# Sparse attention and an FFN on one core: the small attention matmuls issued in six orders of blocks and heads

## The chip, the cores and the metric

The kernel runs on one core of a Trainium2 chip. Its time is the device time in microseconds, the median of several runs. Five engines work side by side, each through its own stream in order: TensorE (matrix products, PE in the profile, with PEld for its weight loads), VectorE (DVE), ScalarE (ACT), GpSimd (POOL) and SyncE (SP, which here only starts DMAs).

## What is computed

Attention over 8 batches, 8 heads, 576 tokens and 64 dimensions a head, with two sparse masks, and then a layer norm with a feed-forward block:

```python
scores = (q @ k.T) / sqrt(64)
mask_local   = (rel >= 0) & (rel < 32)                 # heads 0 to 3
mask_strided = (rel >= 0) & (pos_k % 32 == pos_q % 32) # heads 4 to 7
attn = softmax(where(mask, scores, -1e9))
x = (attn @ v), heads side by side: 8 x 576 x 512
xn = (x - mean(x)) / sqrt(var(x) + 1e-6) * g_ln
out = x + max(xn @ w_ch1, 0) @ w_ch2                   # 512 -> 2048 -> 512
```

## The kernel before

The tokens are worked in nine chunks of 512: one for each batch, and a ninth for the 64 last tokens of all batches. A chunk's FFN is 16 steps (f = 0 to 15). In each step `ffn1` (L748, L755) makes 128 hidden units by 512 tokens, ScalarE and VectorE split them in two parts (`h_high`, `h_low`), and `second` (L775) adds their products into four output banks. The steps are skewed: between `ffn1` of step f and `second` of step f - 1 there is a place for other work on TensorE.

The heads come in pairs, 32 of them, two heads of the same mask in a pair: strided and local pairs alternate. Only the blocks that the mask leaves are computed. A local pair has 18 blocks of 32 queries for each head, a strided pair 11 blocks of three strides (54 queries) for each head. The two heads of a pair lie on different rows of TensorE's array (head 0 on rows 0 to 63, head 1 on rows 64 to 127), and neighbouring blocks of one head on different columns: four groups of 32 columns for local blocks, two groups of 64 for strided ones, used in turn (`tile_position` in L445 and L515). All are plain float32 matmuls; each stands as two load and matmul pairs in TensorE's stream.

Batches 0 and 1 are worked ahead of and within chunk 0, by an order written out by hand (`ORDER`). From chunk 1 on a generator, `pieces`, brings the other 24 pairs, one at every fourth FFN step. Its first part is `m_piece` (L670): in one bank tile `m` of 1536 columns it issues the scores of the next pair (`s_blocks`, L451 to L453, matmul L445), then the v products of this pair (`v_blocks`, L546 to L548, matmul L515). These are called a visit here. VectorE then masks the scores and divides the products, and DMAs carry the softmax weights out and back for the visit after. Both loops run over blocks outside and the two heads inside:

```python
            for i in range(n):
                for h in range(2):
                    block(i, h)
```

The order of instructions within an engine is the order in which the program is written; TensorE's stream is fixed by it.

Of the kernel before, what the change touches and what calls it, by code (L numbers as in the profile page):

```python
# [20 lines left out]
T:0:0:0 T:0:1:1 c:0:0: c:0:1: T:1:0:2 S:0::0 c:1:0: T:1:1:2 mask:0 max:0 T:2:1:0 c:1:1: sub:0  # L21
S:1::1 c:2:1: exp:0 T:2:0:2 mask:1 max:1 PP:0::0 c:2:0: T:3:0:1 sub:1 pt:0 c:3:0: V:0::2 exp:1
vs:1 S:2::0 den:0 xo:0 PP:1::1 mask:2 X:0::2 pt:1 max:2 W:0 T:3:1:0 xh:0 sub:2 V:1::1 xl:0 c:3:1:
S:3::2 den:1 r:4 xo:1 low:0:0 sc:0:0 low:0:1 exp:2 mg:0:0 mask:3 PP:2::1 X:1::0 pt:2 sg:0:0 W:1
max:3 xh:1 V:2::2 sc:0:1 xl:1 sub:3 tp:4 byg:0 exp:3 W:2 PP:3::0 add:0 den:2 S:4::1 pt:3 mg:0:1
vs:3 xo:2 cm:0::0 low:1:0 X:2::2 W:3 mask:4 sg:0:1 V:3::1 xh:2 max:4 sc:1:0 cen:0 sub:4 xl:2 r:5
hi:0:0 lowA:2:0 mg:1:0 hi:0:1 lo:0:0 F:0 exp:4 den:3 sg:1:0 lowA:3:0 lo:0:1 xo:3 sc:1:1 low:1:1
byg:1 X:3::1 mg:1:1 v:4 sg:1:1 add:1 PP:4::2 xh:3 sc:2:0 xl:3 cm:1::0 mg:2:0 Fb:0 pt:4 lowA:3:1
W:4 cen:1 H:0 lowA:2:1 sg:2:0 hi:1:0 tp:5 byg:2 V:4::0 hh:0 sc:2:1 add:2 hl:0 S:5::1 hi:1:1 st:1
mg:2:1 lo:1:0 cm:2::2 sg:2:1 F:1 W:5 mask:5 sc:3:0 lo:1:1 hi:2:1 cen:2 H:1 mg:3:0 hi:2:0 G:0  # L30
sg:3:0 hh:1 den:4 W:6 sc:3:1 hl:1 lowA:4:1 mg:3:1 lo:2:0 byg:3 lowA:4:0 F:2 sg:3:1 add:3 xo:4
sc:4:0 hi:3:1 W:7 mg:4:0 H:2 lo:2:1 lowA:5:0 sg:4:0 cm:3::0 G:1 cen:3 byg:4 sc:4:1 hi:3:0 mg:4:1
add:4 hh:2 sg:4:1 st:4 hl:2 sc:5:0 X:4::0 lo:3:0 F:3 mg:5:0 xh:4 r:6 lo:3:1 lowA:5:1 xl:4 H:3
sg:5:0 cm:4::0 hh:3 G:2 cen:4 byg:5 sc:5:1 hl:3 lowA:6:1 v:5 add:5 mg:5:1 hi:4:0 sg:5:1 lowA:6:0
lo:4:0 F:4 max:5 sc:6:0 lowA:7:0 mg:6:0 sub:5 lowA:7:1 cm:5::0 sg:6:0 H:4 cen:5 W:8 sc:6:1 byg:6
G:3 hh:4 mg:6:1 add:6 hi:4:1 hl:4 hi:5:0 sg:6:1 lo:5:0 cm:6::0 sc:7:0 F:5 cen:6 W:9 exp:5 lo:4:1
mg:7:0 hi:5:1 sg:7:0 H:5 tp:6 byg:7 sc:7:1 PP:5::0 lowA:8:0 G:4 add:7 st:0 hh:5 hi:6:0 hl:5 lo:5:1
pt:5 r:7 mg:7:1 hi:6:1 S:6::0 lo:6:0 sg:7:1 lowA:9:0 lowA:8:1 F:6 mask:6 sc:8:0 max:6 cm:7::0
mg:8:0 sg:8:0 sub:6 H:6 st:3 G:5 hh:6 cen:7 byg:8 st:2 hl:6 hi:7:0 lo:6:1 tp:7 sc:8:1 hi:7:1
V:5::0 add:8 lowA:9:1 r:8 F:7 mg:8:1 sg:8:1 lo:7:0 den:5 sc:9:0 xo:5 H:7 mg:9:0 sg:9:0 cm:8::0  # L40
hh:7 G:6 exp:6 byg:9 hl:7 W:10 sc:9:1 cen:8 add:9 mg:9:1 hi:8:0 PP:6::0 hi:8:1 sg:9:1 lo:8:0 F:8
tp:8 pt:6 W:11 lo:7:1 hi:9:1 cm:9::0 H:8 lo:8:1 sc:10:0 cen:9 lowA:10:0 G:7 lowA:10:1 mg:10:0 W:12
hi:9:0 sg:10:0 hh:8 byg:10 sc:10:1 hl:8 S:8::0 lowA:11:0 lo:9:0 mg:10:1 F:9 lowA:11:1 sg:10:1 v:6
add:10 mask:8 sc:11:0 H:9 mg:11:0 lo:9:1 lowA:12:1 sg:11:0 cm:10::0 G:8 hh:9 cen:10 byg:11 W:13
sc:11:1 hi:10:0 mg:11:1 hi:10:1 lo:10:0 hl:9 lowA:12:0 S:7::0 sg:11:1 add:11 sc:12:0 F:10 mask:7
W:14 lo:10:1 mg:12:0 cm:11::0 sg:12:0 H:10 max:7 sc:12:1 byg:12 G:9 hh:10 cen:11 st:5 add:12
mg:12:1 hi:11:0 hl:10 lowA:13:1 W:15 lo:11:0 sg:12:1 hi:11:1 cm:12::0 F:11 max:8 sc:13:0 lowA:13:0
cen:12 H:11 mg:13:0 hi:12:0 v:7 sg:13:0 lo:12:0 X:5::0 hh:11 G:10 xh:5 lo:11:1 sc:13:1 xl:5
lowA:14:1 hl:11 sub:7 hi:12:1 mg:13:1 V:6::0 lowA:14:0 r:9 byg:13 F:12 sg:13:1 den:6 add:13 xo:6
sc:14:0 H:12 lo:12:1 lowA:15:0 mg:14:0 exp:7 cm:13::0 sg:14:0 G:11 hi:13:1 cen:13 byg:14 xr:0  # L50
hh:12 sc:14:1 hl:12 lo:13:1 hi:13:0 mg:14:1 X:6::0 lo:13:0 sg:14:1 F:13 xh:6 add:14 xr:1 sc:15:0
xl:6 H:13 sub:8 mg:15:0 cm:14::0 hh:13 G:12 cen:14 xr:2 sg:15:0 hi:14:0 hl:13 byg:15 xs:0 PP:7::0
lo:14:0 F:14 pt:7 tp:9 st:6 lowA:15:1 add:15 sc:15:1 H:14 r:10 cm:15::0 hh:14 G:13 cen:15 exp:8
hl:14 hi:14:1 mg:15:1 hi:15:0 sg:15:1 lo:15:0 V:7::0 hi:15:1 xr:3 F:15 lo:15:1 den:7 xo:7 lo:14:1
xs:2 X:7::0 v:8 H:15 G:14 hh:15 xh:7 hl:15 xl:7 v:9 tp:10 PP:8::0 pt:8 xs:3 st:7 r:11 xs:1
# [9 lines left out]
def kernel(  # L65
# [127 lines left out]
    v_l = [v_local(const.tile([P, 4 * NL, D1], F32, name="v_l")),  # L193
           v_local(early.tile([P, 4 * NL, D1], F32, name="v_l1"))]
    v_s = [v_strided(const.tile([P, 2 * NS, D1], F32, name="v_s")),
           v_strided(early.tile([P, 2 * NS, D1], F32, name="v_s1"))]


# [604 lines left out]
    for p in first:  # L803
        if p.k in BY_DVE:
            p.load_qk(early.tile([P, 2 * S], F32, name=f"raw{p.id}"))
        elif p.k == 0:
            for i in range(2):
                p.load_rows(i, nc.sync, slice(0, 1))
                p.load_rows(i, nc.scalar, slice(1, 2))
        else:  # L810
            p.load_rows(0, nc.sync)
            p.load_rows(1, nc.scalar)
    nc.sync.dma_start(gcol, g_ln.rearrange("(c p) -> p c", p=P))
    for p in first:
        p.load_v(once=True)

# [209 lines left out]
```

## Time and profile before

| | |
|---|---|
| median of 3 runs | 906.24 us (904.66 to 908.40) |
| span of the profiled execution | 907.3 us |
| TensorE busy | 884.9 us, 98% of the span |
| VectorE, ScalarE, GpSimd busy | 435.4, 199.7 and 147.9 us |
| DMA | 102.98 MB, mean 114 GB/s |

The span is the time of the profiled execution from its first to its last instruction. A group of instructions is given with its line of the kernel, engine, operation, what it writes and reads, the shape and a count. For a matmul, "64\*32 64x64" means 64 rows by 32 columns of the array and 64 columns streamed. A matmul's busy time reaches from its start to its modelled end, so that neighbours overlap; a row that merges many gives the first start and the time that they cover together. Rates are best read from one row's start to the next.

### The profile page before, as it was taken

The page shows a single profiled execution, that of the slowest core. Times are in us where ns is not written, and L with a number is a line of the kernel's source. Part 1 is how long each engine was busy: PE and PEld are TensorE (multiplying, and loading weights), DVE is VectorE, ACT ScalarE, POOL GpSimd, SP SyncE. Part 2 cuts the span into 40 slices and gives each one's busy share as a digit, 9 for nine tenths or more (in the row PEclk, how much of TensorE's full clock was granted, in tenths as well). Part 3 has the DMA queues.
Part 4 walks back from the last instruction along what each step waited for, and adds up shares of the span by engine and source line. Part 5 has one row for each costly group of instructions (what it writes and reads, how often), then busy time and mean ns, then how long its engine had stood idle before and what let it go on. Part 6 is the DMA issues. An engine that isn't in the chain of part 4 may idle for free.

```text
span 907.3 us, 18531 instructions
## 1 busy us (share of the span) xinstructions
PE 884.9 (98%) x7606; PEld 728.8 (80%) x7606; DVE 435.4 (48%) x864; ACT 199.7 (22%) x326; POOL 147.9 (16%) x186
## 2 busy tenths in 40 slices
PE   7699999999999999999999999999999999999997
PEld 6578787888888888888888888888888888888885
DVE  2888877544654455445644464445533321132113
ACT  3477663111111111111111111111111111111110
POOL 5477774000100011000100010001000000000000
PEclk8999999999999999999999999999999999999999
DMA  8887886675867575766666665757443230002001
GB/s 166 226 257 179 247 196 114 147 111 119 134 142 109 102 137 120 124 91 141 109 134 93 135 104 141 100 127 124 116 85 91 49 128 0 1 1 93 0 1 47
DMA packets 339621, 102.98 MB, mean 114 GB/s; under 512 B 276944, under 2 KB 331344, under 8 KB 339536
## 3 DMA queue, kind: packets, MB, share of 16 engines
q1 hardware_dynamic: 249920, 85.53, 42.9%
q10 hardware_dynamic: 89616, 16.26, 11.5%
q8 instruction: 60, 0.98, 0.5%
q14 instruction: 25, 0.20, 0.1%
HBM read 74.02 MB, written 27.72 MB: 112 GB/s over the span
## 4 chain that ended last, share of the span: by engine, by line
PE 93%; DMA 2%; DVE 1%; issue 1%; SPq 1%; POOL 1%; ACT 0%; DVEq 0%; POOLq 0%; ACTq 0%
PE po L775 42%; PE ph L748 28%; PE ph L755 14%; PE m L515 2%; PE m L445 2%; DMA s<-in_moe_w_ch_dram 1%; PE t L371 1%; PE s L445 1%; DMA rows<-in_q_dram 1%; PE av L515 1%; SPq L351 1%; PE cm L281 1%; PE px L636 0%; PE pp L501 0%; POOL r L270 0%
## 5 line engine op out<-in xcount | busy, mean ns | idle before, releaser
L775 PE MATMUL po<-w,hh 128*128 128x512 f32 x1152 | 359.2, 393 | 0.0
L765 DVE SCALAR_TENSOR_TENSOR hl<-ph,hh 128x512 fp32r<-128x512 f32 x144 | 99.3, 690 | 367.0 <-ACT hh L760 367.0
L775 PEld LDWEIGHTS po<-w,hh 128*128 128x128 f32 x1152 | 213.4, 188 | 44.8
L748 PE MATMUL ph<-xh,w 128*128 128x512 f32 x576 | 226.0, 392 | 1.4 <-ACT w L294 1.2
L775 PE MATMUL po<-w,hl 128*128 128x512 f32 x576 | 224.5, 390 | 0.0
L748 PE MATMUL ph<-xl,w 128*128 128x512 f32 x576 | 224.5, 390 | 0.0
L760 ACT ACTIVATE hh<-ph 128x512 fp32r<-128x512 f32 x144 | 86.1, 598 | 483.7 <-PE ph L755 469.0
L755 PE MATMUL ph<-xh,w 128*128 128x512 f32 x576 | 155.3, 392 | 0.0
L748 PEld LDWEIGHTS ph<-xh,w 128*128 128x128 f32 x576 | 108.3, 188 | 24.1 <-ACT w L294 1.4
L775 PEld LDWEIGHTS po<-w,hl 128*128 128x128 f32 x576 | 108.1, 188 | 23.1
L755 PEld LDWEIGHTS ph<-xh,w 128*128 128x128 f32 x576 | 108.2, 189 | 22.5 <-POOL w L298 0.2
L748 PEld LDWEIGHTS ph<-xl,w 128*128 128x128 f32 x576 | 108.3, 188 | 22.0
L491 POOL TENSOR_TENSOR sm<-sm,mx 128x648 f32<-128x648 f32 (+1 forms) x32 | 40.6, 1269 | 440.4 <-DVE mx L486 440.4
L723 POOL TENSOR_TENSOR rs<-rs,mhalf 128x1 f32<-128x1 f32 x36 | 19.7, 548 | 286.5 <-DVE rs L722 286.5
L497 ACT ACTIVATE sm<-sm 128x648 f32<-128x648 f32 (+1 forms) x32 | 23.8, 742 | 104.3 <-POOL sm L491 104.3
L298 POOL TENSOR_TENSOR w<-r,w 128x512 fp32r<-128x512 f32 x32 | 41.1, 1297 | 7.3 <-ACT w L294 6.9
L687 DVE TENSOR_TENSOR xl<-xo,xh 128x512 fp32r<-128x512 f32 x24 | 16.6, 692 | 38.8 <-ACT xh L686 38.8
L686 ACT ACTIVATE xh<-xo 128x512 fp32r<-128x512 f32 x24 | 15.2, 632 | 62.0 <-DMA pd<-sm 18.2
L486 DVE TENSOR_REDUCE mx<-sm 128x12 f32<-128x648 f32 (+1 forms) x32 | 26.3, 822 | 2.1
L565 DVE TENSOR_TENSOR xo<-m,den 64x64 f32<-64x64 f32 (+3 forms) x120 | 27.1, 289 | 0.0
L781 DVE SCALAR_TENSOR_TENSOR x<-po,rs,x 128x512 f32<-128x512 f32 x36 | 24.5, 737 | 2.0 <-PE po L775 1.8
L718 DVE BATCH_NORM_STATS2 st<-x 128x6 f32<-128x512 f32 x36 | 24.3, 674 | 0.0
(95 smaller groups left out, 561.0 us busy)
## 6 DMA issues: line engine op xcount, KB each, us to landing
s<-in_moe_w_ch_dram SPq DMA_DIRECT2D x32, 512.0 KB
out_dram<-x SPq DMA_DIRECT2D x32, 256.0 KB
raw<-in_q_dram SPq DMA_DIRECT2D x112, 72.0 KB
raw<-in_k_dram SPq DMA_DIRECT2D x112, 72.0 KB
xds<-xo SPq DMA_DIRECT2D x32, 162.0 KB
v_l<-in_v_dram SPq DMA_DIRECT2D x32, 144.0 KB
pd<-sm SPq DMA_DIRECT2D x44, 96.0 KB
pt<-pd ACTq DMA_DIRECT2D x44, 96.0 KB
```

Source lines behind the costliest of these rows:

```text
L298: nc.gpsimd.tensor_tensor(out=t[:, 1], in0=self.w[i], in1=t[:, 0].bitcast(F32), op=ALU.subtract)
L445: nc.tensor.matmul(o, lhsT, rhs, start=True, stop=True, tile_position=(64 * h, pos))
L486: nc.vector.reduce_max(mx[:, :, 0:nt], sm, axis=AX.X)
L491: nc.gpsimd.tensor_tensor(out=sm, in0=sm, in1=mx[:, :, 0:nt].unsqueeze(3).broadcast_to([P, 2, nt, sm.shape[3]]), op=ALU.subtract)
L515: nc.tensor.matmul(at(h, t)[m * j:m * (j + 1)], self.p_cols(rows, t, j), self.v[rows, n, 0:w], start=True, stop=True, tile_position=(64 * ...
L565: nc.vector.tensor_tensor(out=xo[r, t0:t1, h0:h1].rearrange("p t h d -> p h t d"), in0=av, in1=den[r, h0:h1, t0:t1].unsqueeze(3).broadcast_to(
L748: nc.tensor.matmul(ph, w1h[:, cc], x[:, cc, :], start=(new and n == 0 and i == 0), stop=False)
L755: nc.tensor.matmul(ph, w1l[:, cc], xt[c][0][:, cc, :], start=False, stop=(cc == NCC - 1))
L760: nc.scalar.activation(out=hh, in_=ph, func=AF.Relu)
L765: nc.vector.scalar_tensor_tensor(out=hl, in0=ph, scalar=0.0, in1=hh.bitcast(F32), op0=ALU.max, op1=ALU.subtract)
L775: nc.tensor.matmul(po[i], hx[:, cs], w, start=(f == 0 and n == 0), stop=(f == NFC - 1 and n == 2))
L781: nc.vector.scalar_tensor_tensor(out=x, in0=po[i], scalar=rs, in1=x, op0=ALU.mult, op1=ALU.add)
```

## The change

A function `turns(n, kind)` gives the order of the visits to (block, head) in one of six kinds, and the two loops go by it. The kind follows from the number of the pair: visits 0 and 1 have kind 0, visits 2 and 3 kind 1, and so on; after kind 5 it starts again, so that each kind has four of the 24 visits. Kind 0 is the order before. Kind 1 takes two blocks of head 0 and then the same two of head 1; kind 2 alternates heads and crosses the blocks; kind 3 takes four and four; kind 4 all blocks of head 0 and then all of head 1; in kind 5 head 1 follows two blocks behind head 0. Batches 0 and 1 keep kind 0.

```diff
+    def turns(n, kind):
+
+        g = (1, 2, 2, 4, n, 1)[kind]
+        if kind == 5:
+            return [x for i in range(n + 2) for x in ((i, 0), (i - 2, 1)) if 0 <= x[0] < n]
+        out = []
+        for i in range(0, n, g):
+            js = range(i, min(i + g, n))
+            if kind == 2 and len(js) == 2:
+                out += [(i, 0), (i + 1, 1), (i + 1, 0), (i, 1)]
+            else:
+                out += [(j, h) for h in range(2) for j in js]
+        return out
...
-            for i in range(n):
-                for h in range(2):
-                    block(i, h)
+            for i, h in turns(n, (self.k - 9) // 2 % 6 if wide or ps.shape[1] > 1024 else 0):
+                block(i, h)
...
-            for i in range(NB if self.local else NG):
-                for h in range(2):
-                    self.v_block(i, h, lambda h, t: ps[:, o(h, t):o(h, t) + D], D)
+            for i, h in turns(NB if self.local else NG, (self.k - 8) // 2 % 6):
+                self.v_block(i, h, lambda h, t: ps[:, o(h, t):o(h, t) + D], D)
```

The rest of the diff turns the first loads and memsets, which stood as plain lines, into words of `ORDER` at the same place, and gives some steps a choice of engine that no word uses. The other engines' instructions stand in the same order and number as before; so do TensorE's groups of instructions, and what moves is inside a visit. It can be seen where a wait marks a block.

TensorE, visit 8 (the first of kind 4), before: the scores of a local pair and the v products of a strided one, with the FFN's matmuls around them (`m` is the bank tile, `pt` the softmax weights, `v_s` the values, DMAHW the landing of DMAs):

```order
L755 MATMUL ph_0_4151<-xh_3391,w_0_831 128x512 x4
L445 MATMUL m_2_4168<-kt_l,qt_l 32x64 [waits PE_49]
L445 MATMUL m_2_4168<-kt_l,qt_l 32x64 x35
L515 MATMUL m_2_4168<-v_s,pt_2_4088 64x64 [waits DMAHW5_49,DMAHW6_49,DMAHW3_49,DMAHW1_49]
L515 MATMUL m_2_4168<-v_s,pt_2_4088 64x64 [waits DMAHW2_49,DMAHW0_49]
L515 MATMUL m_2_4168<-v_s,pt_2_4088 64x64 [waits DMAHW7_49,DMAHW5_49]
L515 MATMUL m_2_4168<-v_s,pt_2_4088 64x64 x19
```

The same visit now:

```order
L461 MATMUL m_2_4168<-kt_l,qt_l 32x64 x35
L529 MATMUL m_2_4168<-v_s,pt_2_4088 64x64 [waits DMAHW5_49,DMAHW6_49,DMAHW3_49,DMAHW1_49]
L529 MATMUL m_2_4168<-v_s,pt_2_4088 64x64 [waits DMAHW7_49,DMAHW5_49]
L529 MATMUL m_2_4168<-v_s,pt_2_4088 64x64 x9
L529 MATMUL m_2_4168<-v_s,pt_2_4088 64x64 [waits DMAHW2_49,DMAHW0_49]
L529 MATMUL m_2_4168<-v_s,pt_2_4088 64x64 x10
```

Head 1's first block, the one with the wait for DMAHW2 and 0, stood second and stands twelfth, behind all of head 0's.

TensorE, visit 9 (the second of kind 4), before: the scores of a strided pair, the v products of a local one, and the first FFN matmul after them (`kt_s`, `qt_s` hold k and q):

```order
L445 MATMUL m_0_4404<-kt_s,qt_s 64x54 x21
L515 MATMUL m_0_4404<-v_l,pt_0_4339 32x64 [waits DMAHW4_49]
L515 MATMUL m_0_4404<-v_l,pt_0_4339 32x64 [waits DMAHW6_49]
L515 MATMUL m_0_4404<-v_l,pt_0_4339 32x64 x34
L775 MATMUL po_0_4308<-w_3_1071,hh_3_4371 128x512 [waits Activation_49]
```

And now:

```order
L461 MATMUL m_0_4404<-kt_s,qt_s 64x54 x21
L529 MATMUL m_0_4404<-v_l,pt_0_4339 32x64 [waits DMAHW4_49]
L529 MATMUL m_0_4404<-v_l,pt_0_4339 32x64 x17
L529 MATMUL m_0_4404<-v_l,pt_0_4339 32x64 [waits DMAHW6_49]
L529 MATMUL m_0_4404<-v_l,pt_0_4339 32x64 x17
L798 MATMUL po_0_4308<-w_3_1071,hh_3_4371 128x512 [waits Activation_49]
```

The block with the wait for DMAHW6 is head 1's first: it stood second and stands nineteenth.

## Rows read from the trace of the kernel before

**Rows 1.** The page: busy time by engine, and the last chain's shares.
```profile
PE 884.9 (98%) x7606; PEld 728.8 (80%) x7606; DVE 435.4 (48%) x864; ACT 199.7 (22%) x326; POOL 147.9 (16%) x186
...
PE 93%; DMA 2%; DVE 1%; issue 1%; SPq 1%; POOL 1%; ACT 0%; DVEq 0%; POOLq 0%; ACTq 0%
```

**Rows 2.** Busy time in chunks 1 to 6: stretch, length, engines, clock, DMA.
```profile
153.00:703.00 550.00, 550.00 (x4959) 452.58 (x4957) 275.55 (x573) 87.45 (x140) 41.25 (x45) 1.00 0.64 118
```

**Rows 3.** Timeline of TensorE, three visits: start, busy us, line, operation, count.
```profile
156.12 0.92 PE L515 MATMUL m<-v_s,pt 54*64 54x64 f32 x44
156.96 0.74 PE L775 MATMUL po<-w,hh 128*128 128x512 f32 x2
...
416.83 0.91 PE L445 MATMUL m<-kt_s,qt_s 64*64 64x54 f32 x44
417.67 0.97 PE L515 MATMUL m<-v_l,pt 64*32 64x64 f32 x72
418.57 0.73 PE L775 MATMUL po<-w,hh 128*128 128x512 f32 x2
...
440.56 0.97 PE L445 MATMUL m<-kt_l,qt_l 64*32 64x64 f32 x72
441.46 1.07 PE L515 MATMUL m<-v_s,pt 54*64 54x64 f32 x44
442.46 0.74 PE L775 MATMUL po<-w,hh 128*128 128x512 f32 x2
```

**Rows 4.** Groups of TensorE by form, 153 to 703 us: the visits' matmuls.
```profile
L515 PE MATMUL m<-v_s,pt 54*64 54x64 f32 x528 | 12.1, 223 | 0.0
L445 PE MATMUL m<-kt_l,qt_l 64*32 64x64 f32 x864 | 11.7, 224 | 0.0
L515 PE MATMUL m<-v_l,pt 64*32 64x64 f32 x864 | 11.7, 224 | 0.0
L445 PE MATMUL m<-kt_s,qt_s 64*64 64x54 f32 x484 | 10.0, 222 | 0.0
```

**Rows 5.** Timeline, loads, windows from 416.8 to 416.88, 416.90, 417.11 and 417.40.
```profile
416.83 0.15 PEld L445 LDWEIGHTS m<-kt_s,qt_s 64*64 64x64 f32 x4 [0.35 <-issue]
416.83 0.20 PEld L445 LDWEIGHTS m<-kt_s,qt_s 64*64 64x64 f32 x7 [0.35 <-issue]
416.83 0.38 PEld L445 LDWEIGHTS m<-kt_s,qt_s 64*64 64x64 f32 x20 [0.35 <-issue]
416.83 0.68 PEld L445 LDWEIGHTS m<-kt_s,qt_s 64*64 64x64 f32 x40 [0.35 <-issue]
```

**Rows 6.** Timeline, matmuls, windows from 440.5 to 440.62, 440.80, 440.88 and 441.20.
```profile
440.56 0.29 PE L445 MATMUL m<-kt_l,qt_l 64*32 64x64 f32 x8
440.56 0.46 PE L445 MATMUL m<-kt_l,qt_l 64*32 64x64 f32 x32
440.56 0.48 PE L445 MATMUL m<-kt_l,qt_l 64*32 64x64 f32 x33
440.56 0.84 PE L445 MATMUL m<-kt_l,qt_l 64*32 64x64 f32 x65
```

**Rows 7.** Timeline, q's transposes: loads to 25.83 and 25.87, then all matmuls.
```profile
25.79 0.14 PEld L371 LDWEIGHTS t<-ident,rows 96*64 96x64 f32 x2 [0.17 <-DVE sm L473]
25.79 0.20 PEld L371 LDWEIGHTS t<-ident,rows 96*64 96x64 f32 x4 [0.17 <-DVE sm L473]
...
25.79 1.21 PE L371 MATMUL t<-ident,rows 96*64 96x96 f32 x24
26.93 0.45 PE L515 MATMUL av<-v_l,pt 64*32 64x65 f32 x28
```

**Rows 8.** Full-array transposes in the timeline; L515's wait instructions (min/median/max ns).
```profile
25.02 0.85 PE L636 MATMUL px<-ident,xo 128*128 128x128 f32 x6 [0.38 <-DVE xo L565]
...
L515 PEldq EVENT_SEMAPHORE  x68: 51/51/1436, 21.1 to 698.4; - x68
```

More of the change, by code (lines that the diff above doesn't have):

```diff
@@ L20 @@
 ORDER = """
[L21 to L55, printed above, removed]
-"""
-BY_DVE = ()
@@ L59 @@
-ONCE = False
+vm R:0:0 R:0:1 R:1:0 R:1:1:1 R:2:0 R:2:1:1 R:3:0 R:3:1:1 g:0 v:0 v:1 v:2 v:3 T:0:0:0 T:0:1:1 c:0:0:
+c:0:1: T:1:0:2 S:0::0 c:1:0: T:1:1:2 mask:0 max:0 T:2:1:0 c:1:1: sub:0 S:1::1 c:2:1: exp:0 T:2:0:2
+mask:1 max:1 PP:0::0 c:2:0: T:3:0:1 sub:1 pt:0 c:3:0: V:0::2 exp:1 vs:1 S:2::0 den:0 xo:0 PP:1::1
+mask:2 X:0::2 pt:1 max:2 W:0 T:3:1:0 xh:0 sub:2 V:1::1 xl:0 c:3:1: S:3::2 den:1 r:4 xo:1 low:0:0
+sc:0:0 low:0:1 exp:2 mg:0:0 mask:3 PP:2::1 X:1::0 pt:2 sg:0:0 W:1 max:3 xh:1 V:2::2 sc:0:1 xl:1
@@ new lines @@
+sub:3 tp:4 byg:0 exp:3 W:2 PP:3::0 add:0 den:2 S:4::1 pt:3 mg:0:1 vs:3 xo:2 cm:0::0 low:1:0 X:2::2
+W:3 mask:4 sg:0:1 V:3::1 xh:2 max:4 sc:1:0 cen:0 sub:4 xl:2 r:5 hi:0:0 lowA:2:0 mg:1:0 hi:0:1 lo:0:0
+F:0 exp:4 den:3 sg:1:0 lowA:3:0 lo:0:1 xo:3 sc:1:1 low:1:1 byg:1 X:3::1 mg:1:1 v:4 sg:1:1 add:1
+PP:4::2 xh:3 sc:2:0 xl:3 cm:1::0 mg:2:0 Fb:0 pt:4 lowA:3:1 W:4 cen:1 H:0 lowA:2:1 sg:2:0 hi:1:0 tp:5
+byg:2 V:4::0 hh:0 sc:2:1 add:2 hl:0 S:5::1 hi:1:1 st:1 mg:2:1 lo:1:0 cm:2::2 sg:2:1 F:1 W:5 mask:5
@@ new lines @@
+sc:3:0 lo:1:1 hi:2:1 cen:2 H:1 mg:3:0 hi:2:0 G:0 sg:3:0 hh:1 den:4 W:6 sc:3:1 hl:1 lowA:4:1 mg:3:1
+lo:2:0 byg:3 lowA:4:0 F:2 sg:3:1 add:3 xo:4 sc:4:0 hi:3:1 W:7 mg:4:0 H:2 lo:2:1 lowA:5:0 sg:4:0
+cm:3::0 G:1 cen:3 byg:4 sc:4:1 hi:3:0 mg:4:1 add:4 hh:2 sg:4:1 st:4 hl:2 sc:5:0 X:4::0 lo:3:0 F:3
+mg:5:0 xh:4 r:6 lo:3:1 lowA:5:1 xl:4 H:3 sg:5:0 cm:4::0 hh:3 G:2 cen:4 byg:5 sc:5:1 hl:3 lowA:6:1
+v:5 add:5 mg:5:1 hi:4:0 sg:5:1 lowA:6:0 lo:4:0 F:4 max:5 sc:6:0 lowA:7:0 mg:6:0 sub:5 lowA:7:1
+cm:5::0 sg:6:0 H:4 cen:5 W:8 sc:6:1 byg:6 G:3 hh:4 mg:6:1 add:6 hi:4:1 hl:4 hi:5:0 sg:6:1 lo:5:0
@@ new lines @@
+cm:6::0 sc:7:0 F:5 cen:6 W:9 exp:5 lo:4:1 mg:7:0 hi:5:1 sg:7:0 H:5 tp:6 byg:7 sc:7:1 PP:5::0
+lowA:8:0 G:4 add:7 st:0 hh:5 hi:6:0 hl:5 lo:5:1 pt:5 r:7 mg:7:1 hi:6:1 S:6::0 lo:6:0 sg:7:1 lowA:9:0
+lowA:8:1 F:6 mask:6 sc:8:0 max:6 cm:7::0 mg:8:0 sg:8:0 sub:6 H:6 st:3 G:5 hh:6 cen:7 byg:8 st:2 hl:6
+hi:7:0 lo:6:1 tp:7 sc:8:1 hi:7:1 V:5::0 add:8 lowA:9:1 r:8 F:7 mg:8:1 sg:8:1 lo:7:0 den:5 sc:9:0
+xo:5 H:7 mg:9:0 sg:9:0 cm:8::0 hh:7 G:6 exp:6 byg:9 hl:7 W:10 sc:9:1 cen:8 add:9 mg:9:1 hi:8:0
+PP:6::0 hi:8:1 sg:9:1 lo:8:0 F:8 tp:8 pt:6 W:11 lo:7:1 hi:9:1 cm:9::0 H:8 lo:8:1 sc:10:0 cen:9
@@ new lines @@
+lowA:10:0 G:7 lowA:10:1 mg:10:0 W:12 hi:9:0 sg:10:0 hh:8 byg:10 sc:10:1 hl:8 S:8::0 lowA:11:0 lo:9:0
+mg:10:1 F:9 lowA:11:1 sg:10:1 v:6 add:10 mask:8 sc:11:0 H:9 mg:11:0 lo:9:1 lowA:12:1 sg:11:0
+cm:10::0 G:8 hh:9 cen:10 byg:11 W:13 sc:11:1 hi:10:0 mg:11:1 hi:10:1 lo:10:0 hl:9 lowA:12:0 S:7::0
+sg:11:1 add:11 sc:12:0 F:10 mask:7 W:14 lo:10:1 mg:12:0 cm:11::0 sg:12:0 H:10 max:7 sc:12:1 byg:12
+G:9 hh:10 cen:11 st:5 add:12 mg:12:1 hi:11:0 hl:10 lowA:13:1 W:15 lo:11:0 sg:12:1 hi:11:1 cm:12::0
+F:11 max:8 sc:13:0 lowA:13:0 cen:12 H:11 mg:13:0 hi:12:0 v:7 sg:13:0 lo:12:0 X:5::0 hh:11 G:10 xh:5
@@ new lines @@
+lo:11:1 sc:13:1 xl:5 lowA:14:1 hl:11 sub:7 hi:12:1 mg:13:1 V:6::0 lowA:14:0 r:9 byg:13 F:12 sg:13:1
+den:6 add:13 xo:6 sc:14:0 H:12 lo:12:1 lowA:15:0 mg:14:0 exp:7 cm:13::0 sg:14:0 G:11 hi:13:1 cen:13
+byg:14 xr:0 hh:12 sc:14:1 hl:12 lo:13:1 hi:13:0 mg:14:1 X:6::0 lo:13:0 sg:14:1 F:13 xh:6 add:14 xr:1
+sc:15:0 xl:6 H:13 sub:8 mg:15:0 cm:14::0 hh:13 G:12 cen:14 xr:2 sg:15:0 hi:14:0 hl:13 byg:15 xs:0
+PP:7::0 lo:14:0 F:14 pt:7 tp:9 st:6 lowA:15:1 add:15 sc:15:1 H:14 r:10 cm:15::0 hh:14 G:13 cen:15
@@ L60 @@
+exp:8 hl:14 hi:14:1 mg:15:1 hi:15:0 sg:15:1 lo:15:0 V:7::0 hi:15:1 xr:3 F:15 lo:15:1 den:7 xo:7
+lo:14:1 xs:2 X:7::0 v:8 H:15 G:14 hh:15 xh:7 hl:15 xl:7 v:9 tp:10 PP:8::0 pt:8 xs:3 st:7 r:11 xs:1
+"""
 EARLY_F0 = True
@@ L191, in v_strided, with v_frames @@
         return t
[L193 to L196, printed above, removed]
+    v_l = [const.tile([P, 4 * NL, D1], F32, name="v_l"),
+           early.tile([P, 4 * NL, D1], F32, name="v_l1")]
+    v_s = [const.tile([P, 2 * NS, D1], F32, name="v_s"),
+           early.tile([P, 2 * NS, D1], F32, name="v_s1")]
+    def v_frames():
+        for t in v_l:
+            v_local(t)
+        for t in v_s:
+            v_strided(t)
     sms = [const.tile([P, NS, 2, 64], F32, name=f"sm{i}") for i in range(2)]
@@ L266, in sign, with by_g, block_sum @@
                 in1=self.p[i].bitcast(U32), op0=ALU.bitwise_and, op1=ALU.bitwise_or)
-        def by_g(self):
+        def by_g(self, eng):
             self.wg = self.w[0].rearrange("p (c f) -> p c f", c=NCC)
-            nc.gpsimd.tensor_tensor(
+            eng.tensor_tensor(
                 out=self.wg, in0=self.wg, in1=gcol.unsqueeze(2).broadcast_to([P, NCC, P]),
                 op=ALU.mult)
-        def block_sum(self):
-            nc.gpsimd.tensor_tensor(
+        def block_sum(self, eng):
+            eng.tensor_tensor(
                 out=bsum, in0=self.wg[:, 0:2], in1=self.wg[:, 2:4], op=ALU.add)
-            nc.gpsimd.tensor_tensor(out=bsum[:, 0], in0=bsum[:, 0], in1=bsum[:, 1], op=ALU.add)
+            eng.tensor_tensor(out=bsum[:, 0], in0=bsum[:, 0], in1=bsum[:, 1], op=ALU.add)
         def column_mean(self, ps):
@@ L294, in high, with rest @@
             nc.scalar.activation(out=t[:, 0], in_=self.w[i], func=AF.Copy)
-        def rest(self, i):
+        def rest(self, i, eng):
             t = (w1s, w2s)[i][self.f]
-            nc.gpsimd.tensor_tensor(
+            eng.tensor_tensor(
                 out=t[:, 1], in0=self.w[i], in1=t[:, 0].bitcast(F32), op=ALU.subtract)
@@ L316 @@
     NHP = H // 2
+    CC = 2
     CT = 96
-    NA = S // CT // 2
+    NA = S // (CT * CC)
     n_pair = [0, 0]
+    def turns(n, kind):
[10 more added lines that the diff above has]
+        return out
     class Pair:
@@ L358, in load_rows @@
             if self.rows is None:
-                self.rows = early.tile([CT, 2, 2, NA, 2, D], F32, name=f"rows{self.id}")
+                self.rows = early.tile([CT, 2, 2, NA, CC, D], F32, name=f"rows{self.id}")
             src = (q, k)[i]
@@ L363, in load_rows @@
                 src[self.b, self.h0 + hs.start:self.h0 + hs.stop].rearrange(
-                    "h (a p c) d -> p (h a) (c d)", p=CT, c=2))
+                    "h (a p c) d -> p (h a) (c d)", p=CT, c=CC))
         def t_rows(self, i, ps):
@@ L368, in t_rows @@
             for a in range(NA):
-                for c in range(2):
+                for c in range(CC):
                     for h in range(2):
@@ L374, in t_rows, with t_copy @@
             self.t_ps[i] = ps[:, :, 0:2 * CT]
-        def t_copy(self, i):
+        def t_copy(self, i, copy):
             self.qt, self.kt = (qt_l, kt_l) if self.local else (qt_s, kt_s)
@@ L379, in t_copy @@
             if self.local:
-                nc.scalar.copy(
-                    out=dst[:, STR * i:STR * i + S].rearrange("p (a x) -> p a x", a=NA), in_=ps)
-            else:
-                nc.scalar.copy(
-                    out=dst[:, 0:S].rearrange("p (r a u) -> p a u r", a=NA, r=STR),
-                    in_=ps.rearrange("p a (u r) -> p a u r", r=STR))
+                copy(out=dst[:, STR * i:STR * i + S].rearrange("p (a x) -> p a x", a=NA), in_=ps)
+            else:
+                copy(out=dst[:, 0:S].rearrange("p (r a u) -> p a u r", a=NA, r=STR),
+                     in_=ps.rearrange("p a (u r) -> p a u r", r=STR))
         def load_v(self, once=False):
@@ L487, in s_max, with s_sub @@
             self.mx = mx
-        def s_sub(self):
+        def s_sub(self, eng=nc.gpsimd):
             nt, sm, mx = self.nt, self.smv, self.mx
-            nc.gpsimd.tensor_tensor(
+            eng.tensor_tensor(
                 out=sm, in0=sm,
@@ L501, in p_turn, with p_copy @@
                 nc.tensor.transpose(pp[:, P * t:P * (t + 1)], self.sm[:, t].rearrange("p h x -> p (h x)"), ident)
-        def p_copy(self, pp):
+        def p_copy(self, pp, copy):
             pool, tag = (early, f"pt{self.k % 2}") if self.b == 0 else (smp, "pt")
             pt = pool.tile([P, NS, P], F32, tag=tag, name=f"pt{self.id}")
-            nc.scalar.copy(
-                out=pt[:, 0:self.nt].rearrange("p t x -> p (t x)"), in_=pp[:, 0:P * self.nt])
+            copy(out=pt[:, 0:self.nt].rearrange("p t x -> p (t x)"), in_=pp[:, 0:P * self.nt])
             w = STR if self.local else 64
@@ L595, in x_raw, with x_turned, x_blocks, p_turned @@
                     self.xraw[32 * j:32 * j + 32].rearrange("p (g e) -> p g e", e=32), src)
-        def x_blocks(self):
-            xh, xl = x_t(self.b)
-            cc = self.h0 // 2
+        def x_turned(self):
             xT = self.xo.rearrange("p t h d -> p (t h d)")[:, 0:CH]
             nc.vector.transpose(xT, self.xraw)
-            split_x(xh[:, cc, :], xl[:, cc, :], xT)
-        def p_turned(self):
-            nt = self.nt
-            turned = sms[1 - int(self.local)].rearrange("p t h x -> p (t h x)")[
-                :, 0:P * nt].rearrange("p (b t e) -> p b t e", b=4, e=32)
+            cc = self.h0 // 2
+            self.xp = [(xT, *(x[:, cc, :] for x in x_t(self.b)))]
+        def x_blocks(self):
+            self.x_turned()
+            for src, hi, lo in self.xp:
+                split_x(hi, lo, src)
+        def p_turned(self, own=False):
+            nt = self.nt
+            if own:
+                turned = smp.tile([P, NS, P], F32, tag="pt", name=f"turned{self.id}").rearrange(
+                    "p t x -> p (t x)")
+            else:
+                turned = sms[1 - int(self.local)].rearrange("p t h x -> p (t h x)")
+            turned = turned[:, 0:P * nt].rearrange("p (b t e) -> p b t e", b=4, e=32)
             nc.vector.transpose(
@@ L616, in p_turned, with p_load @@
                     turned[32 * j:32 * j + 32].rearrange("p b t e -> p b (t e)"))
-        def p_load(self):
+        def p_load(self, dma=nc.scalar.dma_start):
             nt, src = self.nt, pd[int(self.local)]
@@ L622, in p_load @@
                 ptj = pt.rearrange("p t x -> p (t x)")[:, 0:P * nt]
-                nc.scalar.dma_start(ptj, src.rearrange("p j x -> p (j x)"))
+                dma(ptj, src.rearrange("p j x -> p (j x)"))
                 ptj = ptj.rearrange("p (j t e) -> p j t e", j=4, e=32)
@@ L627, in p_load @@
                 for j in range(4):
-                    nc.scalar.dma_start(
+                    dma(
                         pt[:, 0:nt, 32 * j:32 * j + 32],
@@ L658, in x_parts, with x_high @@
             return [(src, dst(xh), dst(xl)) for src, dst in parts]
-        def x_high(self, px):
-            self.xp = self.x_parts(px)
+        def x_high(self, px=None):
+            if px is not None:
+                self.xp = self.x_parts(px)
             for src, hi, _ in self.xp:
@@ L802 @@
     first = pairs[0:NHP]
[L803 to L815, printed above, removed]
     NP = len(pairs)
@@ L843, in one @@
         p = pairs[k]
-        if op == "T":
+        eng, copy = nc.gpsimd, nc.scalar.copy
+        if op.endswith("D"):
+            op, eng, copy = op[0:-1], nc.vector, nc.vector.tensor_copy
+        if op == "R":
+            if k == 0:
+                p.load_rows(i, nc.sync, slice(0, 1))
+                p.load_rows(i, nc.scalar, slice(1, 2))
+            else:
+                p.load_rows(i, nc.scalar if buf else nc.sync)
+        elif op == "vm":
+            v_frames()
+        elif op == "Z":
+            t = room(f"d{len(ps)}", buf - 1) if buf else wake
+            for _ in range(k):
+                nc.tensor.matmul(
+                    t[:, 0:2 * P].rearrange("p (n x) -> p n x", x=P), mean,
+                    mean.unsqueeze(1).broadcast_to([P, 2, P]), start=True, stop=True)
+        elif op == "g":
+            nc.sync.dma_start(gcol, g_ln.rearrange("(c p) -> p c", p=P))
+        elif op == "T":
             p.t_rows(i, room(f"t{k}{i}", buf))
         elif op == "c":
-            p.t_copy(i)
+            p.t_copy(i, copy)
         elif op == "S":
@@ L854, in one @@
         elif op == "sub":
-            p.s_sub()
+            p.s_sub(eng)
         elif op == "exp":
@@ L860, in one @@
         elif op == "pt":
-            p.p_copy(ps[f"pp{k}"])
+            p.p_copy(ps[f"pp{k}"], copy)
         elif op == "vs":
@@ L874, in one @@
         elif op == "xh":
-            p.x_high(ps[f"px{k}"])
+            p.x_high(ps.get(f"px{k}"))
         elif op == "xl":
             p.x_low()
+        elif op == "pT":
+            p.p_turned(bool(i))
+        elif op == "pL":
+            p.p_load(nc.sync.dma_start)
+        elif op == "xr2":
+            p.x_raw(nc.sync)
+        elif op == "xT":
+            p.x_turned()
         elif op == "tp":
@@ L882, in one @@
         elif op == "v":
-            p.load_v(once=ONCE)
+            p.load_v(once=p.b == 0)
         elif op == "W":
@@ L896, in one @@
         elif op == "byg":
-            split(k).by_g()
+            split(k).by_g(eng)
         elif op == "add":
-            split(k).block_sum()
+            split(k).block_sum(eng)
         elif op == "cm":
@@ L906, in one @@
         elif op == "lo":
-            split(k).rest(i)
+            split(k).rest(i, eng)
         elif op == "F":
```

## The prediction

> **What bounds the kernel now.** I read the chain of work that ended last first: TensorE holds 93% of it [rows 1]. The table by stretches then shows chunks 1 to 6, from 153 to 703 us: TensorE is busy for 550.00 of 550 us, VectorE for half of it, and the granted clock is 1.00, its 2.4 GHz level [rows 2]. In that stage no wait ends last but TensorE's own work, so whatever the change adds to TensorE's stream there is added to the end, and whatever it takes off is taken off. The change touches only the small matmuls of attention. They come in 24 visits of TensorE, one between two halves of each FFN step, and the timeline shows a visit as two rows [rows 3]: the scores of the next pair (L445), then the v products of this pair (L515). Two kinds of block alternate. A "strided" half has 11 blocks for each of two heads, each on 64 rows and 64 columns of the array; a "local" half has 18 for each head on 64 rows and 32 columns. Each float32 block is issued as two load and matmul pairs, so that 22 blocks are x44 and 36 are x72. From row to row a strided half takes 0.84 us (1.00 in most v halves), a local one 0.90 [rows 3]. All 2,740 of these matmuls are 45.5 us of busy time [rows 4]: that is the whole stake, and an order can move a part of it only.
>
> **What paces a visit.** How fast blocks follow each other must be read within a half. In a strided half four loads start, two blocks, one of each head; then nothing starts until between 416.88 and 416.90, some 55 ns after the first at 416.83 [rows 5]. From then on it goes in that step: 20 loads have started by 417.11 and 40 by 417.40, which is 20 loads, five pairs of blocks, in 0.29 us or 58 ns for a pair [rows 5]. Two loads of different heads (other rows of the array) follow within 7 ns or so; the next block of the same head waits 58. In a local half the same step is half as long: 8 matmuls (two blocks of each head) start within 0.06 us, 32 by 0.24 [rows 6], 28 ns for a block of one head. After the 32nd only one starts in the next 0.08 us, and then 32 take 0.32 us [rows 6]: there something other than the array, most likely the supply of instructions, sets the pace at 36 ns for a pair of blocks.
>
> So a head moves on by one block in 58 ns (strided) or 28 ns (local), and the order before runs both heads side by side. Would two blocks of one head also overlap if they are neighbours in the stream? The rows before have one nearby case, the transposes of q and k at L371: their neighbours take the same rows and differ in columns, like block j and block j+1 of one head. Two loads of the first block start at 25.79, and the next two only between 25.83 and 25.87 [rows 7], again the length of one load. A matmul behind a load that cannot start is not passed by others, as far as these rows show: I take it that the stream stops at a block whose head is still loading the block before, even when the block after it belongs to the free head.
>
> **The change, order by order.** Each order serves visits 0 and 1, 2 and 3, and so on, twice in all; two neighbouring visits hold two strided and two local halves, so each order has four of each (order 5 three strided ones, since the last visit has no scores). The order listing shows it where waits mark the blocks: in the first visit of order 4 the wait that head 1's first v block carries moves from the second v block to the twelfth, behind all of head 0. I price a half by its neighbours: 58 (28) ns for a block of the same head as the one before, 14 ns (two pairs at 7) for a block of the other head, and 45 (14) for the last block, whose step no other hides. Before, that gives 11 x 58 = 0.64 us for a strided half; a local one takes the measured 0.75 (0.90 less the 0.15 of changing over, which stays).
> - Order 0 is the order before: 0.
> - Order 1 (two of one head, two of the other): strided 10 x 58 + 12 x 14 + 45 = 0.79, so +0.15; local 18 x 28 + 18 x 14 + 14 = 0.77, so +0.02. Four of each: 0.68 us.
> - Order 2 (heads alternate, columns cross): the heads still alternate, so 0; the odd last block of a strided half meets a column in use, 0 to 58 ns, taken at 30. Four: 0.12 us.
> - Order 3 (four and four): strided 16 x 58 + 6 x 14 + 45 = 1.06, +0.42; local 26 x 28 + 10 x 14 + 14 = 0.88, +0.13. Four of each: 2.2 us.
> - Order 4 (one head, then the other): strided 20 x 58 + 2 x 14 + 45 = 1.23, +0.59; local 34 x 28 + 2 x 14 + 14 = 0.99, +0.24. Four of each: 3.3 us.
> - Order 5 (head 1 two blocks behind): two more steps, 2 x 58 = +0.12 in three strided halves; local 20 x 28 = 0.56 stays under the 0.75 that the supply sets, +0 to 0.05. Together 0.45 us.
>
> The sum is 6.8 us. What works against it: v halves of strided pairs take up to 0.16 us more than the first of them (1.00 against 0.84) [rows 3], since their first blocks wait for several loads, 51 ns for each extra wait instruction [rows 8]; in the head-by-head orders part of these stand behind queued blocks, which I price at 0 to 0.6 us over the kernel and take at 0.3. Below nothing the sum can't go by more than the same waits, 12 such halves at some 0.1 each, 1.2 us. Nothing covers the rest: VectorE reads the scores and products later, but has half of its time free [rows 2], and the next visit is 24 us away. Matmuls of the FFN, DMA queues and the other engines keep their order. The forecast is +6.5 us. The profiled span of 907.3 would become 913.8; it lies 1.0 over the median of 906.24, so the median would become 912.7 (0.7% slower).
>
> **Where a rule differs.** The rows of L371 show 12 blocks, x24, from 25.79 to 26.93 [rows 7]: 1.14 us with the change of mode, 95 ns or less for a block of two passes, though all share the array's rows. The Trainium skill's page "TensorE: Matmul & The Clock Gate", in its part on packing small matmuls under "The mechanism", says that a weight load overlaps running matmuls only when its row group differs. By that rule neighbours of one head would not overlap at all; it is the third rival, and these rows speak against it in that strict form.
>
> **The rivals.**
> (a) TensorE looks past a waiting block. Place: the runs of one head in orders 1, 3 and 4. If it can hold some four loads of one head and go on to the other, orders 1 and 3 cost almost nothing (0.1 and 0.5 us) and order 4 still some 2.9 (its two heads then overlap only around the middle), together about 3.5 us; if it looks past a whole head (22 loads), all is 0. It decides from there: at four loads held the time is 909.7, within 0.5%, and at 22 it is 906.2, not slower. For it: after a stop several loads start at once. Against it: the stop after two blocks in [rows 5] and [rows 7].
> (b) The supply, not the array, is what counts, and spreading the waits frees it: orders 1 to 5 cost nothing and the strided v halves gain, down by the 1.2 us above to 905.0 (no change, as far as can be measured). The 58 ns step of strided halves, slower than the supply's 36, speaks against it.
> (c) Neighbours of one head don't overlap at all. The nearest price is a full-array block, x6 in 0.85 us with its start, about 110 ns a pass, 220 for two [rows 8]. Orders 1, 3, 4 have 46 such neighbours in their strided halves and 78 in the local ones, four times each, near 500 in all, each some 190 ns dearer: 95 us, to about 1,000.
> (d) The clock. Visits of order 4 last about 1 us longer with half of the array idle; if the granted clock fell to its 1.2 GHz level after each of four, some 3 us of matmuls at half speed each, it would cost 6 to 12 us more, 919 to 925. At 1.00 throughout [rows 2] with visits of 2 us, nothing points to it.
> That the change doesn't do what it says is excluded by the listing of instructions.
>
> **How the numbers follow.** Forecast 0.66, with its own range of 909.5 to 915.5: the steps by a tenth each way, the waits from 0 to 1.2 us, and 1.5 us of scatter (the runs of before reach from 904.66 to 908.4). Rival (a) 0.24, (b) 0.03, (c) 0.02, (d) 0.05. For 8 in 10 the range takes in the forecast's and the upper half of (a): 907.8 to 915.8. A change under 0.5%, 4.5 us, can't be told from none here. Of the forecast about nine tenths lie over 910.8, with (c) and (d) 0.66 for slower; 0.32 within, from (a), (b) and the rest of the forecast; 0.02 for faster, which only scatter on top of (b) would give.
>
> **What would show it.** In the timeline after, row to row: strided halves of order 4 at 1.45 us and of order 3 at 1.25 where now 0.84 stands, local ones at 1.15 and 1.03 for 0.90, order 2 unchanged, order 1 at 1.0 for strided halves. TensorE's busy time per stretch would stay full, and FFN rows keep 0.39 us each. If orders 3 and 1 cost nothing and order 4 does, (a) is right; if all six stand alike, the step of 58 ns was not a head's own. Forecast and sum are wrong if TensorE's other rows move at all, since then a clock or a wait has entered.

## The result, and the profile after

The change made the kernel a little slower: 912.78 us median against 907.32 for the kernel before in the same comparison, ratio 1.0062 (95% interval 1.004 to 1.0085). That is the time that was forecast, 912.7. The trace says that it was reached by another way than the one worked out.

The page of the changed kernel, busy time by engine, and the table by stretches for chunks 1 to 6 (here the lines are L461 for scores and L529 for v products):

```profile
PE 890.2 (98%) x7606; PEld 733.8 (81%) x7606; DVE 436.1 (48%) x864; ACT 199.7 (22%) x326; POOL 147.7 (16%) x186
```
```profile
153.00:706.00 553.00, 553.00 (x4889) 455.62 (x4888) 276.27 (x573) 87.17 (x139) 41.24 (x45) 1.00 0.64 118
```

TensorE is still busy throughout, at a granted clock of 1.00, as in [rows 2], and the FFN's matmuls keep their mean of 389 to 393 ns. What the visits cost is in the groups by form, from 153 to 707 us:

```profile
L529 PE MATMUL m<-v_s,pt 54*64 54x64 f32 x528 | 13.6, 223 | 0.0
L529 PE MATMUL m<-v_l,pt 64*32 64x64 f32 x864 | 12.0, 223 | 0.0
L461 PE MATMUL m<-kt_l,qt_l 64*32 64x64 f32 x864 | 12.0, 223 | 0.0
L461 PE MATMUL m<-kt_s,qt_s 64*64 64x54 f32 x484 | 11.2, 222 | 0.0
```

Together 48.8 us against 45.5 in [rows 4]: 3.3 us more, where the sum of the prediction had 6.8 and the medians differ by 5.5. Of the 3.3, the four visits of kind 4 have 2.4. The timeline of TensorE, first a visit of kind 1, then kinds 2, 3, 4 (two visits) and 5:

```profile
227.14 0.91 PE L461 MATMUL m<-kt_s,qt_s 64*64 64x54 f32 x44
227.98 0.97 PE L529 MATMUL m<-v_l,pt 64*32 64x64 f32 x72
...
274.83 0.92 PE L461 MATMUL m<-kt_s,qt_s 64*64 64x54 f32 x44
275.68 0.97 PE L529 MATMUL m<-v_l,pt 64*32 64x64 f32 x72
...
322.42 0.95 PE L461 MATMUL m<-kt_s,qt_s 64*64 64x54 f32 x44
323.31 0.97 PE L529 MATMUL m<-v_l,pt 64*32 64x64 f32 x72
324.21 0.50 PE L798 MATMUL po<-w,hh 128*128 128x512 f32 x1
...
346.21 1.12 PE L461 MATMUL m<-kt_l,qt_l 64*32 64x64 f32 x72
347.26 1.43 PE L529 MATMUL m<-v_s,pt 54*64 54x64 f32 x44
348.62 0.50 PE L798 MATMUL po<-w,hh 128*128 128x512 f32 x1
...
370.60 1.41 PE L461 MATMUL m<-kt_s,qt_s 64*64 64x54 f32 x44
371.95 1.13 PE L529 MATMUL m<-v_l,pt 64*32 64x64 f32 x72
373.01 0.50 PE L798 MATMUL po<-w,hh 128*128 128x512 f32 x1
...
418.94 0.95 PE L461 MATMUL m<-kt_s,qt_s 64*64 64x54 f32 x44
419.81 0.97 PE L529 MATMUL m<-v_l,pt 64*32 64x64 f32 x72
```

From row to row, where [rows 3] have 0.84 for strided scores: kind 1 0.84, kind 2 0.85, kind 3 0.89, kind 4 1.35, kind 5 0.87. Local halves stay at 0.90 in all kinds but 4, where they take 1.05 and 1.06. So in these halves runs of two and four blocks of one head cost next to nothing, and only whole heads one after the other cost much. The 0.9 us that isn't kind 4's lies mostly in the strided v products of kinds 1, 2, 3 and 5, 0.03 to 0.33 us each, where waits for DMAs and the order of blocks come together.

Why can be seen in how the loads begin. Scores of a visit of kind 3 (windows to 322.44 and 322.463) and of one of kind 4 (to 370.65 and 370.67):

```profile
322.42 0.14 PEld L461 LDWEIGHTS m<-kt_s,qt_s 64*64 64x64 f32 x2 [0.35 <-issue]
322.42 0.16 PEld L461 LDWEIGHTS m<-kt_s,qt_s 64*64 64x64 f32 x4 [0.35 <-issue]
...
370.60 0.14 PEld L461 LDWEIGHTS m<-kt_s,qt_s 64*64 64x64 f32 x2 [0.35 <-issue]
370.60 0.20 PEld L461 LDWEIGHTS m<-kt_s,qt_s 64*64 64x64 f32 x4 [0.35 <-issue]
```

Both streams begin with blocks of head 0: four in kind 3, eleven in kind 4. Both begin with the same blocks, so the first eight loads are the same. In kind 4 the third load comes after some 50 ns or more, the step of [rows 5]. In kind 3 four loads have begun after 43 ns. One head doesn't give more than two in that time, as kind 4 shows, so the third and fourth must be head 1's, whose first load stands ninth in the stream: it went past six loads of head 0 that were still waiting. The rows don't name the head; that part is inferred. At the change of heads in kind 4 (windows to 371.10 and 371.14) it was fewer:

```profile
370.60 0.60 PEld L461 LDWEIGHTS m<-kt_s,qt_s 64*64 64x64 f32 x18 [0.35 <-issue]
370.60 0.66 PEld L461 LDWEIGHTS m<-kt_s,qt_s 64*64 64x64 f32 x22 [0.35 <-issue]
```

The first 18 loads came at the pace of one head. Then four begin within 0.04 us, more than one head gives, so that here head 1's joined in while about four of head 0's 22 were waiting.

### The profile page after: what moved, and what is told of

Same layout as the page of the kernel before. It is cut to its first block, busy times and chain, and to the rows that moved or that the text cites. A ratio compares the mean times of both kernels' runs of the same rounds, so it can differ in the third digit from the quotient of the medians.

```text
span 911.0 us, 18530 instructions
## 1 busy us (share of the span) xinstructions
PE 890.2 (98%) x7606; PEld 733.8 (81%) x7606; DVE 436.1 (48%) x864; ACT 199.7 (22%) x326; POOL 147.7 (16%) x186
## 4 chain that ended last, share of the span: by engine, by line
PE 91%; DMA 4%; SPq 2%; DVE 2%; POOL 1%; issue 0%; DVEq 0%; ACT 0%; POOLq 0%; ACTq 0%
PE po L798 42%; PE ph L771 28%; PE ph L778 14%; PE m L529 3%; PE m L461 2%; DMA s<-in_moe_w_ch_dram 2%; DMA rows<-in_q_dram 2%; SPq L369 1%; SPq L417 0%; PE cm L284 0%; POOL r L273 0%; SPq L227 0%; PE px L658 0%; DVE x L804 0%; SPq L230 0%
```

## The experiments

Two theories: the prediction's step, that the stream stops at a block whose head is loading; and rival (a), that some loads can wait aside while later ones of another head go on.

**Kind 0 everywhere, and the change once more.** The control keeps the new program and sets kind 0 in all visits:

```diff
-            for i, h in turns(n, (self.k - 9) // 2 % 6 if wide or ps.shape[1] > 1024 else 0):
+            for i, h in turns(n, 0 if wide or ps.shape[1] > 1024 else 0):
...
-            for i, h in turns(NB if self.local else NG, (self.k - 8) // 2 % 6):
+            for i, h in turns(NB if self.local else NG, 0):
```

> The changed program with kind 0 in all 24 visits, so that only the new way of writing it is left. The trace of the change shows 3.3 us more in the 24 visits (the sum of row to row differences), while the medians differ by 5.5. If the other 2.2 us are scatter of the first 153 us, this kernel stands within 1 us of the kernel before (ratio 0.999 to 1.001) and every visit keeps its time. If they come with the new program itself, it is 2 us slower, 1.002.

> The change itself, timed again beside the control. Scatter theory: +3.3 us, ratio 1.0036. A steady cost outside of the visits: +5.5 us, ratio 1.006.

Measured: the control 907.42 against 906.61, ratio 1.0002 (0.999 to 1.0014), with every half of its visits as before within the scatter of the waits. The change itself, now timed beside it, 910.08, ratio 1.0036 (1.0022 to 1.005). So the new program by itself costs nothing that can be told (-0.9 to 1.3 us), the reorder costs 3.3 us by the ratio (2.0 to 4.5), the 3.3 of the trace, and the other 2 us of the first comparison are best put down to scatter. The profiles show where scatter lies: in the stretch before the first visit. The first visit of the control and of the kernel with kind 3 everywhere (below), whose programs up to that place are the same, then of two executions of the change (spans 911.0 and 908.3 us), then of the kernel before (907.3):

```profile
152.55 0.97 PE L461 MATMUL m<-kt_l,qt_l 64*32 64x64 f32 x72
```
```profile
157.40 0.97 PE L461 MATMUL m<-kt_l,qt_l 64*32 64x64 f32 x72
```
```profile
155.76 0.97 PE L461 MATMUL m<-kt_l,qt_l 64*32 64x64 f32 x72
```
```profile
153.16 0.97 PE L461 MATMUL m<-kt_l,qt_l 64*32 64x64 f32 x72
```
```profile
155.22 0.97 PE L445 MATMUL m<-kt_l,qt_l 64*32 64x64 f32 x72
```

The first two lie 4.9 us apart, and the two executions of the change 2.6, of 2.7 in their spans. Counted from the first visit's start to the end of the span, which leaves that stretch out, it is 752.1 us before and in the control, 755.2 and 755.1 with the change.

**Kind 4 everywhere, kind 3 everywhere.** The same edit as above with 4 and with 3 for the 0.

> Kind 4 (all blocks of one head, then the other) in all 24 visits. Prediction's step (the stream stops at a block whose head is still loading): +0.59 us for a strided and +0.24 for a local half, 23 and 24 halves or so, 19 to 20 us. Lookahead of about four loads (rival a), from the visits of kind 4 in the trace of the change, which take 0.49 to 0.53 us more with local scores and 0.67 with strided ones: 12 x 0.51 + 11 x 0.67 + 0.16 = 13.6 us. If the granted clock falls in these visits, more than 20 us and a clock below 1.00.

> Kind 3 (four blocks of a head, then four of the other) in all 24 visits. Prediction's step: +0.42 us for a strided half and +0.13 for a local one, 12 to 13 us in all. Lookahead of about four loads: +0.05 for strided scores, 0 for local halves, and 0.1 to 0.33 for strided v products, whose first blocks wait for loads: 2 to 4.5 us. The two differ by 8 us.

Measured: kind 4 921.74 us, ratio 1.0156 (1.0136 to 1.0175), 14.1 us by the ratio, where lookahead gave 13.6 and the step 19 to 20. Kind 3 909.85 us, ratio 1.0028 (1.0015 to 1.0042), 2.5 us, where lookahead gave 2 to 4.5 and the step 12 to 13. The 13.6 was added up from the visits of kind 4 in the trace of the change, so that its coming true shows that these visits repeat, not how far the lookahead goes. The first visit with kind 4 everywhere (that of kind 3 stands above, at 157.40):

```profile
154.70 1.12 PE L461 MATMUL m<-kt_l,qt_l 64*32 64x64 f32 x72
```

From the first visit to the end of the span (920.9 and 911.0) kind 4 takes 14.1 and kind 3 1.5 us more than the kernel before. So by the trace kind 3 costs a little less than the 2 to 4.5 expected of lookahead. The step, which had its price at least five times too large, is refuted by it. The groups of the kernel with kind 3 show where its small price lies:

```profile
L529 PE MATMUL m<-v_s,pt 54*64 54x64 f32 x528 | 13.0, 223 | 0.0
L461 PE MATMUL m<-kt_l,qt_l 64*32 64x64 f32 x864 | 11.7, 224 | 0.0
L529 PE MATMUL m<-v_l,pt 64*32 64x64 f32 x864 | 11.7, 224 | 0.0
L461 PE MATMUL m<-kt_s,qt_s 64*64 64x54 f32 x484 | 10.5, 223 | 0.0
```

Against [rows 4]: strided v products +0.9 us (under 0.1 a half, where the expectation had 0.1 to 0.33), strided scores +0.5, local halves 0. The clock stayed at 1.00 in these stages, with kind 4 too, which takes rival (d) away.

**Runs of six.** In kind 3 everywhere, six for four:

```diff
-        g = (1, 2, 2, 4, n, 1)[kind]
+        g = (1, 2, 2, 6, n, 1)[kind]
```

> Six blocks of head 0, then six of head 1 (strided: six and five), in all visits: it measures how far TensorE goes on past a busy head. Strided scores took 0.688 us from first to last start with heads alternating, +0.05 with runs of four and +0.51 with runs of eleven. A queue that holds four waiting loads of a head and then stops gives about +0.2 (in a small model of that rule, which gives +0.06 for runs of four and +0.52 for eleven), one of eight loads +0.07, one of two loads +0.39. The prediction's step (no lookahead): 15 x 58 + 4 x 14 + 45 less 640, +0.33. Local halves: 0 up to eight loads, since the supply of instructions still sets their 0.756.

One run: 911.8 us against 906.9 beside it, and 4.4 us more than before from the first visit's start (153.54) to the end of the span (910.0). The strided scores and local v products of its second visit, and the loads of these scores in windows to 177.69 and 177.72:

```profile
177.53 1.07 PE L461 MATMUL m<-kt_s,qt_s 64*64 64x54 f32 x44
178.53 1.01 PE L529 MATMUL m<-v_l,pt 64*32 64x64 f32 x72
179.48 0.50 PE L798 MATMUL po<-w,hh 128*128 128x512 f32 x1
...
177.53 0.25 PEld L461 LDWEIGHTS m<-kt_s,qt_s 64*64 64x64 f32 x6 [0.35 <-issue]
177.53 0.31 PEld L461 LDWEIGHTS m<-kt_s,qt_s 64*64 64x64 f32 x10 [0.35 <-issue]
```

Strided 1.00 from row to row, +0.16; local 0.95, +0.05, which no theory had. The strided price lies between that of four waiting loads (+0.2) and of eight (+0.07), so about five or six by the model. The loads agree: after six, two at a time, four begin within 0.03 us, so head 1's have joined in while about five of head 0's twelve were waiting. With the six of kind 3 and the four of kind 4, TensorE goes past four to six loads in these halves; what sets the number was not tried.

**Column by column.** Heads alternate as before, but the blocks go through one group of columns before the next, in all visits (the numbers in the two loops are 0 as in the control):

```diff
+        m = 4 if n > 12 else 2
+        if kind == 0 and n < 20:
+            return [(i, h) for c in range(m) for i in range(c, n, m) for h in range(2)]
         g = (1, 2, 2, 4, n, 1)[kind]
```

> Heads alternate as before, but the blocks go column by column: strided 0, 2, 4 ... 10 and then 1, 3 ... 9; local 0, 4, 8, 12, 16, then 1, 5 ... Neighbours of a head now share rows and columns of the array. If the 58 ns step belongs to a head's rows, nothing changes: 0.69 and 0.76 us. If the unit is the tile of rows and columns, which takes its blocks' two loads one after the other (2 x 58 ns for a strided block), a strided half takes 0.2 to 0.55 us more and a local one 0.4 to 1.2, the less the more the next column is begun ahead.

One run: 931.78 us against 906.86, 24.9 us more, the dearest of all orders. The edit reaches the strided scores of batches 0 and 1 too, ahead of the visits (8.0 us busy for 5.2 in the control); the first visit starts at 153.08 all the same, and from there to the end of the span (930.0) it is 24.8 us more than before. Its second visit:

```profile
177.92 1.31 PE L464 MATMUL m<-kt_s,qt_s 64*64 64x54 f32 x44
179.16 1.64 PE L532 MATMUL m<-v_l,pt 64*32 64x64 f32 x72
180.73 0.50 PE L801 MATMUL po<-w,hh 128*128 128x512 f32 x1
```

Strided 1.24 (+0.40), local 1.57 (+0.67), both within what the tile theory gave; heads alternate here, so a step that belongs to a head's rows would have cost nothing. The loads of the strided half, in windows to 178.25 and 178.31, now come two in 58 ns or so, where [rows 5] have four:

```profile
177.91 0.43 PEld L464 LDWEIGHTS m<-kt_s,qt_s 64*64 64x64 f32 x12 [0.35 <-issue]
177.91 0.49 PEld L464 LDWEIGHTS m<-kt_s,qt_s 64*64 64x64 f32 x14 [0.35 <-issue]
```

So the unit that is busy is the tile, rows by columns. It takes the two loads of a strided block one after the other, some 117 ns, and the order before keeps four such tiles at work. The 58 ns of a head were two tiles side by side. Local halves have the same step. Loads of a later visit, in windows to 351.87 and 352.09:

```profile
351.77 0.20 PEld L464 LDWEIGHTS m<-kt_l,qt_l 64*32 64x32 f32 x6 [0.35 <-issue]
351.77 0.42 PEld L464 LDWEIGHTS m<-kt_l,qt_l 64*32 64x32 f32 x14 [0.35 <-issue]
```

Eight loads in 0.22 us are two in 55 ns, where [rows 6] have eight matmuls in 60 ns: all eight tiles were at work there, four for each head, and 28 ns a block was four tiles side by side.

## Why the prediction came out

**Time, direction and range held, the sum didn't.** The forecast of +6.5 us met a first comparison of +5.5, but with more runs the change costs 3.3 us, 0.36%, which is the case of rival (a), forecast at about 3.5 us with a chance of 0.24. By the bound of 0.5% that the prediction set, "no change" is the better description of the effect. That 912.78 fell on 912.7 was luck: a sum twice too large met about 2 us of scatter.

**The step that failed** is "the stream stops at a block whose head is still loading the block before, even when the block after it belongs to the free head". It was taken from [rows 7]. Those transposes use the same 96 rows in every block and two groups of columns in turn: once both were loading, there was no free tile that a later block could have gone to, and the rows couldn't tell a stop from a lack of free work. [rows 5] were misread the same way. The four loads that start are not two blocks of two loads each but the first loads of four blocks, on four tiles, as the column order shows, so that the stop after them, counted against rival (a), only shows that all tiles were busy. The case that could have spoken, a run of one head followed by the other, was in no row before, and the prediction should have kept both ends at even chances. In the terms of the sum, for a strided half of scores: kind 1 +0.15 forecast, 0.00 measured; kind 3 +0.42, 0.05; kind 5 +0.12, 0.03; kind 2 +0.03, 0.01. The largest error is kind 3, 2.2 us of the sum: in its visits some 0.1 for the scores, 0 for local halves and 0.45 for the v products.

**What held.** Kind 4: +0.59 forecast for strided scores, +0.51 measured, since there the lookahead ends and eleven blocks on two tiles must take their time; the lookahead gives only the overlap at the change of heads back. For local halves +0.24 forecast, +0.15 and 0.16 measured. The unit of the pace was named as a head's rows, where it is the tile; in these six kinds both give the same price for a head alone, and only the column order tells them apart. Order 3 and 1 leave local halves at 0.90: these have slack, whatever paces them after the 32nd matmul. That it is the supply of instructions was only argued and was not tried; the 0.05 that local halves lose with runs of six stays open too. The prediction has a visit at each FFN step; it is every fourth, which changes no term.

**The waits.** In kind 4 the strided v products take 1.36 us, 0.01 more than the scores, where [rows 3] have 1.00 against 0.84: the waits of the first blocks are hidden behind queued ones, as forecast. In kinds 3 and 5 a part of them stays; how much of the 0.9 us of kind 3's v products is waits and how much order was not taken apart.

**Rivals.** (a) is what happens, in its form with about four loads. (b) failed: no half became shorter beyond the scatter of the waits. (c) failed by far, as kind 3 shows. (d) failed: the granted clock is 1.00 from 153 to 706 us, and also with kind 4 everywhere (from 153 to 717 us).

## What to carry to other kernels

In this kernel small matmuls on parts of the array run side by side by tile (rows and columns), so neighbours in the stream should lie on different tiles, and as many tiles as there are should come up within a few blocks; which index runs inside mattered little as long as that held. Before pricing an order from a row that seems to show a stop, ask whether that row had any free work that could have gone on. And where an effect is under half a per cent, compare the rows that the change touches: here the trace gave 3.3 us at once, while the first medians gave 5.5.

## What was not expected

TensorE went past six waiting loads of one head to begin the other's (kind 3: four loads begun within 43 ns), and runs of four blocks cost 0.05 us in a half of 0.84. Alternating the heads but staying in one group of columns costs far more than putting whole heads one after the other: 24.9 us against 14.1. The difference is all in the local halves, where the first leaves two of eight tiles at work (+0.67 us) and the second four (+0.15 or so). For strided scores both leave two of four, at +0.40 and +0.51.
